# The branch at the end of a kernel: the skipped transfers go to another queue, and the flag is computed earlier

## The chip, the cores and the metric

The kernel runs on one core of a Trainium2 chip. The metric is device time in microseconds (us). The program is one launch with one execution of straight-line code and, at the very end, one branch on a value computed on the device.

## The reference

A gated recurrence over 6080 steps, then two dense layers with a shrink function between them:

```python
sig = 1.0 / (1.0 + np.exp(-f_logit))
f = lower_bound + (1.0 - lower_bound) * sig
for t in range(S):                      # B=4, S=6080, D=256
    h = f[:, t] * h + (1.0 - f[:, t]) * x[:, t]
    y[:, t] = h
h = y.reshape(B * S, D) @ w_in          # 256 -> 2048
g = h - np.tanh(h)
out = g @ w_out                         # 2048 -> 256
```

## The kernel before

`fast()` computes everything with a polynomial for `h - tanh(h)` that holds for small `h`. While it works, ScalarE adds up in `flags` by how much any `h*h` exceeds a bound. At the end `worst` is the maximum of the flags, a product with a column of ones sums it over the partitions, and the sum goes to `flag`. If it isn't zero, `general()` recomputes the output in full. With the given inputs it is zero and `general()` is skipped. Every engine reads the flag and branches.

```python
def end(j):                                     # the last block, in two halves
    for half, slot, r in ((0, 2, 1), (1, 1, 0)):
        nc.vector.tensor_tensor(...)            # last addition, waits for Qd
        turn_out(j, (slot,))                    # VectorE transpose
        send(j, half)                           # four nc.sync.dma_start of 64 KB

def sum_up():
    most = ps_b.tile([P, 2, HB], FP32, name="most", tag="D")
    nc.tensor.matmul(most[0:1, 0, 0:1], lhsT=worst[:], rhs=ones[:], start=True, stop=True)
    nc.scalar.copy(out=flag[:], in_=most[0:1, 0, 0:1])
...                                             # order of the last unit on TensorE:
                                                # Qa, Qb, Qc, Qd (8, 8, 4, 8 products), then `most`
@with_exitstack
def general(ctx):
    ...
    fetch_w(u, raw[:], nc.sync)                 # 16 loads of weights
    fetch(j)                                    # 8 loads of each of 48 blocks, nc.sync
    nc.sync.dma_start(out=out[...], in_=osb[...])   # one store of each block
...
fast()
seen = nc.values_load(flag[:].bitcast(INT32), ...)  # every engine loads the flag
with tc.If(seen != 0, label="general"):
    general()
```

Of the kernel before, what the change touches and what calls it, by code (L numbers as in the profile page):

```python
# [31 lines left out]
def kernel(  # L32
# [25 lines left out]
    nc = tc.nc  # L58
# [18 lines left out]
    NBLK = len(starts)  # L77
# [81 lines left out]
    def recurrence(ctx):  # L159

        natpool = ctx.enter_context(tc.tile_pool(name="nat", bufs=1))
        midpool = ctx.enter_context(tc.tile_pool(name="mid", bufs=1))
        ypool = ctx.enter_context(tc.tile_pool(name="ypool", bufs=2))
        nats, chan, ys = {}, {}, {}

        def fetch(j, parts=(0, 1)):
            t0, nb = starts[j], sizes[j]
            for s in parts:
                nat = natpool.tile([P, TB // H, KC * H], FP32, name=("fn", "xn")[s])
                src = srcs[s][t0 : t0 + nb, :].rearrange(  # L170
                    "(j b) (i c) -> i b j c", b=H, i=G
                )
                for i in range(G):
                    nc.sync.dma_start(
                        out=nat[i * H : (i + 1) * H, 0 : nb // H, :], in_=src[i]
                    )
                nats[j, s] = nat

        def turn(j, s):

            n = sizes[j] // H
            dst = midpool.tile([P, TB // H, KC, H], FP32, name=("fT", "xT")[s])
            nc.vector.transpose(
                out=dst[:, 0:n].rearrange("p j k b -> p (j k b)"),
                in_=nats[j, s][:, 0:n, :].rearrange("p j (a k) -> p j k a", k=KC),
            )
            chan[j, s] = dst[:, 0:n]

        def squash(j):

            u = chan[j, 0]
            nc.scalar.activation(out=u, in_=u, func=AF.Sigmoid, scale=-1.0)

        def forget(j, k):

            f = midpool.tile([P, TB // H, H], FP32, name="f", tag=f"f{k}")
            nc.scalar.activation(
                out=f[:, 0 : sizes[j] // H], in_=chan[j, 0][:, :, k, :],
                func=AF.Identity, scale=nom[:, k : k + 1], bias=1.0,
            )  # L200
            chan[j, "f", k] = f[:].rearrange("p j b -> p (j b)")

        def enter(j, k):

            v = midpool.tile([P, TB // H, H], FP32, name="v", tag=f"v{k}")
            nc.vector.scalar_tensor_tensor(
                out=v[:, 0 : sizes[j] // H], in0=chan[j, 0][:, :, k, :],
                scalar=om[:, k : k + 1], in1=chan[j, 1][:, :, k, :],
                op0=ALU.mult, op1=ALU.mult,
            )  # L210
            chan[j, "v", k] = v[:].rearrange("p j b -> p (j b)")

        def recur(j, k):


            t0, nb = starts[j], sizes[j]
            if j not in ys:
                ys[j] = ypool.tile([P, KC, TB], FP32, name="y")
            y, f, v = ys[j], chan[j, "f", k], chan[j, "v", k]
            cuts = [c for c in range(1, nb) if (t0 + c) % S == 0]  # L220
            for a, e in zip([0] + cuts, cuts + [nb]):
                if (t0 + a) % S == 0:
                    init = 0.0
                else:
                    pn = sizes[j - 1]
                    init = ys[j - 1][:, k, pn - 1 : pn]
                nc.vector.tensor_tensor_scan(
                    out=y[:, k, a:e], data0=f[:, a:e], data1=v[:, a:e], initial=init,
                    op0=ALU.mult, op1=ALU.add,
                )  # L230

        steps = dict(
            tf=lambda j: turn(j, 0),
            tx=lambda j: turn(j, 1),
            sg=squash,
            f0=lambda j: forget(j, 0),
            f1=lambda j: forget(j, 1),
            v0=lambda j: enter(j, 0),
            v1=lambda j: enter(j, 1),
            sc0=lambda j: recur(j, 0),  # L240
            sc1=lambda j: recur(j, 1),
        )
        return fetch, steps, ys, natpool, midpool, nats, chan

    @with_exitstack
    def fast(ctx):
# [8 lines left out]
        fetch, steps, ys, natpool, midpool, nats, chan = recurrence(ctx)  # L255
# [274 lines left out]
        def end(j):  # L530
# [38 lines left out]
            o3=lambda j: finish(j, 3),  # L569
# [26 lines left out]
        for word in around.split():  # L596
            name, u, at = re.fullmatch(r"([a-zA-Z0-9]+)(?:\.(\d))?([+-]\d)?", word).groups()
# [235 lines left out]
        def sum_up():  # L833

            most = ps_b.tile([P, 2, HB], FP32, name="most", tag="D")
            nc.tensor.matmul(
                most[0:1, 0, 0:1], lhsT=worst[:], rhs=ones[:], start=True, stop=True
            )
            nc.scalar.copy(out=flag[:], in_=most[0:1, 0, 0:1])
# [33 lines left out]
        with tc.manual_schedule():  # L873
            nc.vector.memset(zeros[:], 0.0)
            nc.vector.memset(ones[:], 1.0)
            nc.scalar.dma_start(
                out=lb[:], in_=lower_bound.rearrange("(p k) -> p k", k=KC)
            )
            make_identity(nc, ident[:])

            nc.scalar.activation(out=flag[:], in_=ones[0:1, :], func=AF.Sigmoid)
            nc.scalar.activation(
                out=om[:], in_=lb[:], func=AF.Identity, scale=-1.0, bias=1.0
            )
            nc.scalar.activation(out=nom[:], in_=lb[:], func=AF.Identity, bias=-1.0)
            busy = ps_b.tile([P, TB], FP32, name="B", tag="B")
            open_by(before.split())
            for cycle in range(PLAIN + 1, NBLK + 3):
                for name, u, at in turns:
                    j = cycle + at  # L890
                    if not PLAIN <= j < NBLK:
                        continue
                    if u is None:
                        if (name, j) == ("o1", NBLK - 1):
                            tc.mark_branch_hint_location("general", "LikelyTaken")
                            nc.vector.reduce_max(
                                out=worst[:], in_=flags[:], axis=mybir.AxisListType.X
                            )
                        if j == NBLK - 1 and name in ("o4", "otr"):
                            if name == "o4":  # L900
                                sum_up()
                                end(j)
                            continue
                        steps[name](j)
                        if (name, j) == ("o3", NBLK - 1):
                            turn_out(j, (0, 3))
                        if name == "tx" and j + 1 < NBLK:
                            fetch(j + 1)
                        continue
                    steps[name](j * NU + u)  # L910

    @with_exitstack
    def general(ctx):

        fetch, steps, ys = recurrence(ctx)[0:3]
        wpool = ctx.enter_context(tc.tile_pool(name="w", bufs=1))
# [8 lines left out]
        def temp(tag, dtype=FP32):  # L925
            return tpool.tile([P, 2, 2, HB], dtype, name=tag, tag=tag)

        with tc.manual_schedule():
            for u in range(NU):
                for fetch_w, w in ((fetch_w_in, w_in[u]), (fetch_w_out, w_out[u])):  # L930
                    raw = tpool.tile([P, KC * TB], INT64, name="raw", tag="raw")
                    fetch_w(u, raw[:], nc.sync)
                    rounding = to_float32(
                        [(w[:].rearrange("p a b c -> p (a b c)"), lambda a: a)], raw[:],
                        lambda n: temp(dict(e="t", m="q", r="th")[n])[:].rearrange(
                            "p a b c -> p (a b c)"
                        ),
                    )
                    for step in ("ce", "cr", "cx", "cm", "cs", "cb", "cw"):
                        rounding[step]()  # L940
            for j, nb in enumerate(sizes):
                ns = nb // P
                fetch(j)
                for step in ("tf", "tx", "sg", "f0", "f1", "v0", "v1", "sc0", "sc1"):
                    steps[step](j)
                ps = ps_o.tile([P, NQ, D], FP32, name="psO")
                for u in range(NU):
# [43 lines left out]
                                )  # L991
                osb = opool.tile([P, NQ, D], FP32, name="osb")
                nc.scalar.copy(out=osb[:, 0:ns, :], in_=ps[:, 0:ns, :])
                nc.sync.dma_start(
                    out=out[starts[j] : starts[j] + nb, :].rearrange(
                        "(i p) d -> p i d", p=P
                    ),
# [1 line left out]
                )  # L999

    fast()
    seen = nc.values_load(
        flag[:].bitcast(INT32),
        skip_runtime_bounds_check_because="it is only compared with zero",
    )
    with tc.If(seen != 0, label="general"):
        general()


# [30 lines left out]
```

## Time and profile before

| | before |
|---|---|
| time, median of 3 runs | 2337.45 us (2335.92 to 2338.53) |
| span of the profiled run | 2334.7 us |
| TensorE busy | 2318.4 us, 99% |
| last transpose ends | 11.45 us before the end |
| SyncE's last eight issues | 2322.48 to 2329.72 us, two of them over 2 us long |
| SyncE from its branch to its next instruction | 2.48 us |

The body belongs to TensorE; the last 11 us belong to SyncE. The lines that show it stand in the prediction. A `q` after an engine's name marks an instruction that its sequencer handles, and `L1006` is the line of the branch. SyncE *issues* a transfer with one instruction; the transfer has *landed* when its semaphore, a counter on which others wait, is full. A *semaphore step* raises by hand a semaphore that a skipped transfer would have raised. An *instruction packet* is a packet of the DMA queues that the page marks as `instruction`: in the profile before 85 packets of 16 KB on queue 8 (1.39 MB) and 63 of 8 KB on queue 14 (0.52 MB). One that follows an engine's branch is called that engine's *fetch*. TensorE's branch began at 2322.44 us. `L836` is the line of the flag's product: TensorE's sequencer was at the wait ahead of it at 2318.3 us. At its end the program waits for all semaphores and then goes through *drains* and a barrier of all engines.

### The profile page before, as it was taken

The page shows a single profiled execution, that of the slowest core. Times are in us where ns is not written, and L with a number is a line of the kernel's source. Part 1 is how long each engine was busy: PE and PEld are TensorE (multiplying, and loading weights), DVE is VectorE, ACT ScalarE, POOL GpSimd, SP SyncE. Part 2 cuts the span into 40 slices and gives each one's busy share as a digit, 9 for nine tenths or more (in the row PEclk, how much of TensorE's full clock was granted, in tenths as well). Part 3 has the DMA queues.
Part 4 walks back from the last instruction along what each step waited for, and adds up shares of the span by engine and source line. Part 5 has one row for each costly group of instructions (what it writes and reads, how often), then busy time and mean ns, then how long its engine had stood idle before and what let it go on. Part 6 is the DMA issues. An engine that isn't in the chain of part 4 may idle for free.

```text
span 2334.7 us, 28635 instructions
## 1 busy us (share of the span) xinstructions
PE 2318.4 (99%) x10669; PEld 2024.6 (87%) x10669; DVE 2121.2 (91%) x2450; ACT 1800.4 (77%) x2685; POOL 0.7 (0%) x6
## 2 busy tenths in 40 slices
PE   9999999999999999999999999999999999999997
PEld 6888888888888888888888888888888888888886
DVE  8999899998999999998999989999899998999987
ACT  7677777777777777777777777777777777778774
POOL 0000000000000000000000000000000000000000
PEclk9999999999999999999999999999999999999999
DMA  5211111111111211112111121111211111111101
GB/s 172 63 23 35 39 37 28 28 39 35 37 28 28 45 29 37 28 28 46 31 34 28 28 46 36 28 28 30 44 37 28 28 36 37 37 28 28 28 10 29
DMA packets 298564, 85.05 MB, mean 36 GB/s; under 512 B 292016, under 2 KB 294320, under 8 KB 298416
## 3 DMA queue, kind: packets, MB, share of 16 engines
q1 hardware_dynamic: 298272, 83.14, 16.9%
q8 instruction: 85, 1.39, 0.3%
q14 instruction: 63, 0.52, 0.1%
q10 hardware_dynamic: 144, 0.00, 0.0%
HBM read 58.20 MB, written 24.90 MB: 36 GB/s over the span
## 4 chain that ended last, share of the span: by engine, by line
PE 99%; DMA 0%; SPq 0%; DVE 0%; issue 0%; DVEq 0%
PE A L383 27%; PE Qa L466 14%; PE Qb L466 14%; PE D L383 14%; PE Qd L466 14%; PE Qc L466 7%; PE B L383 7%; PE Qc L745 1%; PE Qa L745 1%; PE Qb L745 1%; PE A L678 1%; PE D L678 0%; PE Qd L678 0%; DMA xn<-in_x_dram 0%; PE B L678 0%; PE Qc L678 0%
## 5 line engine op out<-in xcount | busy, mean ns | idle before, releaser
L383 PE MATMUL A<-T,w_in 128*128 128x256 f32 x2208 | 558.8, 379 | 0.0
L383 PEld LDWEIGHTS A<-T,w_in 128*128 128x128 f32 x2208 | 419.5, 190 | 57.0
L427 DVE TENSOR_TENSOR h<-h,q 128x1024 f32<-128x1024 f32 x368 | 437.3, 1219 | 3.1
L421 DVE SCALAR_TENSOR_TENSOR q<-q,t 128x1024 f32<-128x1024 f32 x368 | 439.8, 1215 | 0.0
L414 ACT ACTIVATE q<-t 128x1024 f32<-128x1024 f32 x368 | 382.9, 1053 | 46.3 <-DVE h L427 43.4
L411 ACT ACTIVATE t<-h 128x1024 f32<-128x1024 f32 x368 | 388.6, 1056 | 3.1 <-DVE h L398 0.3
L432 ACT ACTIVATE junk<-t 128x1024 bf16<-128x1024 f32 x368 | 388.2, 1055 | 1.5
L446 DVE TENSOR_TENSOR Tg<-h 128x1024 f32<-128x1024 f32 x368 | 347.8, 945 | 6.3
L466 PE MATMUL Qb<-h,w_out 128*128 128x256 f32 x1472 | 347.7, 379 | 0.0
L466 PEld LDWEIGHTS Qb<-h,w_out 128*128 128x128 f32 x1472 | 279.7, 190 | 38.0
L466 PE MATMUL Qa<-Tg,w_out 128*128 128x256 f32 x736 | 219.0, 379 | 0.0
L466 PE MATMUL Qd<-Tg,w_out 128*128 128x256 f32 x736 | 218.9, 379 | 0.0
L466 PE MATMUL Qd<-h,w_out 128*128 128x256 f32 x736 | 218.9, 379 | 0.0
L466 PE MATMUL Qa<-h,w_out 128*128 128x256 f32 x736 | 218.9, 379 | 0.0
L395 ACT COPY h<-B 128x512 f32<-128x512 f32 x184 | 107.0, 581 | 143.3 <-PE B L383 94.5
L395 ACT COPY h<-A 128x512 f32<-128x512 f32 x184 | 107.2, 583 | 136.7 <-PE A L383 125.3
L398 DVE TENSOR_TENSOR h<-D,r 128x512 f32<-128x512 f32 x184 | 126.8, 689 | 93.6 <-PE D L383 91.3
L398 DVE TENSOR_TENSOR h<-A,r 128x512 f32<-128x512 f32 x184 | 126.2, 686 | 74.6 <-PE A L383 42.5
L395 ACT COPY r<-A 128x512 f32<-128x512 f32 x184 | 107.2, 583 | 106.0 <-PE A L383 106.0
L383 PE MATMUL B<-y,w_in 128*128 128x256 f32 x736 | 188.9, 379 | 0.0
L383 PE MATMUL D<-y,w_in 128*128 128x256 f32 x736 | 188.9, 379 | 0.0
L383 PE MATMUL A<-y,w_in 128*128 128x256 f32 x736 | 188.9, 379 | 0.0
(114 smaller groups left out, 3068.3 us busy)
## 6 DMA issues: line engine op xcount, KB each, us to landing
xn<-in_x_dram SPq DMA_DIRECT2D x184, 128.0 KB, 3.3
fn<-in_f_logit_dram SPq DMA_DIRECT2D x184, 128.0 KB, 3.2
out_dram<-osb SPq DMA_DIRECT2D x180, 128.0 KB, 2.8
raw<-in_moe_w_in_dram SPq DMA_DIRECT2D x8, 512.0 KB, 5.2
raw<-in_moe_w_out_dram SPq DMA_DIRECT2D x8, 512.0 KB, 4.7
fn<-in_f_logit_dram SPq DMA_DIRECT2D x1, 512.0 KB, 6.6
xn<-in_x_dram SPq DMA_DIRECT2D x1, 512.0 KB, 7.4
out_dram<-osb SPq DMA_DIRECT2D x1, 512.0 KB, 2.9
```

What stands on the lines that cost most here:

```text
L383: nc.tensor.matmul(ps[:, c], lhsT=w_in[u][:, slot, c * P : (c + 1) * P], rhs=mixes[j][right], start=start and c == 0, stop=True, skip_grou ...
L395: nc.scalar.copy(out=dst, in_=piece(n, bank))
L398: nc.vector.tensor_tensor(out=piece(n, "h")[:, q], in0=piece(n, bank), in1=piece(n, r), op=ALU.add)
L411: nc.scalar.activation(out=half(n, i, "t"), in_=half(n, i), func=AF.Square)
L414: nc.scalar.activation(out=half(n, i, "q"), in_=half(n, i, "t"), func=AF.Square, scale=RA, bias=RB,)
L421: nc.vector.scalar_tensor_tensor(out=q, in0=q, scalar=RC, in1=t, op0=ALU.add, op1=ALU.mult)
L427: nc.vector.tensor_tensor(out=h, in0=h, in1=q, op=ALU.mult)
L432: nc.scalar.activation(out=junk[:, :, :, 0 : st[n]["hb"]], in_=t, func=AF.Relu, bias=-TINY, accum_out=flags[:, 2 * n + i : 2 * n + i + 1],)
L446: nc.vector.tensor_tensor(out=o, in0=a, in1=b, op=ALU.subtract)
L466: nc.tensor.matmul(acc[j, part][:, r, 0 : st[n]["hb"]], lhsT=w_out[u][:, slot, c * P : (c + 1) * P], rhs=piece(n, right)[:, q, c], start=( ...
L678: nc.tensor.matmul(h[c], lhsT=w_in[u][:, 2 * k + s, c * P : (c + 1) * P], rhs=ys[j][:, k, 0:nb], start=k == 0 and (c == 0 or len(banks) == 2),
L745: nc.tensor.matmul(acc[j][i // 2][:, i % 2].rearrange("p (k m) -> p k m", k=2), lhsT=plain[j, u][:, s, c, i * P : (i + 1) * P], rhs=w_out[ ...
```

## The change

SyncE is to skip no code: all transfers of `general()` go through GpSimd's queue. The flag is to be known sooner: its product stands ahead of the last eight products of TensorE instead of behind them. The branch hint goes.

```diff
-        def fetch(j, parts=(0, 1)):
+        def fetch(j, parts=(0, 1), queue=nc.sync):
...
-                    nc.sync.dma_start(
+                    queue.dma_start(
...
                         if (name, j) == ("o1", NBLK - 1):
-                            tc.mark_branch_hint_location("general", "LikelyTaken")
                             nc.vector.reduce_max(
...
                             if name == "o4":
-                                sum_up()
                                 end(j)
                             continue
+                        if (name, j) == ("o3", NBLK - 1):
+                            sum_up()
                         steps[name](j)
...
-                    fetch_w(u, raw[:], nc.sync)
+                    fetch_w(u, raw[:], nc.gpsimd)
...
-                fetch(j)
+                fetch(j, queue=nc.gpsimd)
...
-                nc.sync.dma_start(                      # the store of a block in general()
+                nc.gpsimd.dma_start(
...
-    with tc.If(seen != 0, label="general"):
+    with tc.If(seen != 0):
```

## The prediction

> **What bounds the kernel now.** I read the page first. TensorE is busy for the whole span and is nearly the whole chain that ended last, so nothing that leaves TensorE's stream as it is can move the body of the time:
>
> ```profile
> span 2334.7 us, 28635 instructions
> PE 2318.4 (99%) x10669; PEld 2024.6 (87%) x10669; DVE 2121.2 (91%) x2450; ACT 1800.4 (77%) x2685; POOL 0.7 (0%) x6
> PE 99%; DMA 0%; SPq 0%; DVE 0%; issue 0%; DVEq 0%
> ```
>
> The change touches only what comes after the last product, so I then read the chain near its end, and the busy time in short windows:
>
> ```profile
> 2318.92 0.88 PE Qc L466 x4
> ...
> 2322.45 0.32 DVE C L535
> 2322.78 0.02 issue
> 2322.80 0.45 DVE osb L512
> ...
> 2323.30:2326.00 2.70, 0.00 (x0) 0.00 (x0) 0.00 (x0) 0.00 (x0) 0.00 (x0) 0.74 0.30 64
> 2326.00:2330.00 4.00, 0.00 (x0) 0.00 (x0) 0.00 (x0) 0.00 (x0) 0.00 (x0) 0.50 0.37 81
> 2330.00:2334.70 4.70, 0.00 (x0) 0.00 (x0) 0.00 (x0) 0.00 (x0) 0.00 (x0) 0.50 0.10 24
> ```
>
> The chain ends with VectorE's last transpose at 2323.25 us, 11.45 us before the span ends, and in the three windows (length, then busy time of TensorE, its weight loads, VectorE, ScalarE, GpSimd; clock; DMA share; GB/s) no engine computes. These 11.45 us are SyncE's: it issues the last output, looks at the flag, branches, and closes the program. The timeline of its queue (start, duration) shows the issues, and the views of the lines of the branch and of the waits show the rest:
>
> ```profile
> 2322.48 0.32 SPq L521 DMA_DIRECT2D out_dram<-osb  x1
> 2322.85 0.44 SPq L521 DMA_DIRECT2D out_dram<-osb  x1
> 2323.34 2.20 SPq L521 DMA_DIRECT2D out_dram<-osb  x1
> ...
> 2327.09 2.14 SPq L521 DMA_DIRECT2D out_dram<-osb  x1
> 2329.27 0.45 SPq L521 DMA_DIRECT2D out_dram<-osb  x1
> ...
> L1002 SPq TENSOR_LOAD <-flag x1: 487/487/487, 2329.8 to 2329.8; - x1
> ...
> L1006 SPq EVENT_SEMAPHORE  x8: 17/17/17, 2332.8 to 2333.3; - x8
> ...
> L1006 PEldq COMPARE_BRANCH  x1: 4127/4127/4127, 2322.4 to 2322.4; - x1
> ...
> L1006 SPq COMPARE_BRANCH  x1: 45/45/45, 2330.3 to 2330.3; - x1
> ...
> SPq L1006 <- SPq L1006: 2.4, 1, 2.4
> ...
> L836 PEldq EVENT_SEMAPHORE  x1: 51/51/51, 2318.3 to 2318.3; - x1
> ```
>
> The tail adds up, by the trace's records of SyncE: eight issues of 64 KB from 2322.48 to 2329.72; load of the flag 2329.78 to 2330.27; branch to 2330.39; 2.43 us of nothing until its first instruction at the branch's target (2332.82); eight steps of semaphores that the skipped transfers would have raised, 0.07 to 0.08 us apart (to 2333.41); eight waits 0.06 us apart (to 2333.9); drains and the barrier (0.75 us) to 2334.66. The last output's semaphore is full at 2331.13, so its landing is hidden behind the jump.
>
> Two of the eight issues take 2.20 and 2.14 us where others take some 0.45. In the DMA records, queue 8 brings two packets of 16 KB at 2323.47 (1.64 us) and 2327.31 (1.53 us), and each slow issue ends 0.4 us after such a packet (2325.54 after 2325.11; 2329.23 after 2328.84). [...] The first packet begins 0.98 us after TensorE's branch, the second 0.7 us after it goes on.
>
> [...] after their branches SyncE lost 2.43 us, ScalarE 2.80, VectorE 3.01 and TensorE 4.1, with a fetch 0.88 to 0.98 us after each; GpSimd, which has nothing to skip now, went on 0.16 us after its branch began. [...] here queue 14's packets are 8 KB and only queue 8's are 16 KB. [...] its sequencer was already at the wait ahead of the flag's product at 2318.3, behind the dispatch of products that ran until 2321.51.
>
> **The change part by part.** (1) *SyncE skips no code.* All 16 weight loads, the 8 loads per block and the store of `general` go to GpSimd. SyncE's branch should then cost what GpSimd's does now, 0.16 us in place of the 2.48 us from the branch's start to the next instruction: minus 2.3. The eight semaphore steps go as well: minus 0.6. But the landing comes out: it is full at 2331.13, whereas SyncE would be at its waits at 2330.5, so 0.6 is lost there. The semaphore that lands last is third of eight in the closing list: 5 waits of 0.062 remain after it, 0.31, then 0.75 to the end. With issues as now: 2331.13 + 0.03 + 0.31 + 0.75 = 2332.2, minus 2.4.
>
> (2) *The flag earlier.* `sum_up` moves ahead of `Qd` of the last unit. `worst` is ready at 2318.3, and `Qc` ends at 2319.80; the one-column product (0.19 us) and ScalarE's copy (0.15 us) make the flag known at about 2320.15 in place of 2321.83, 1.7 us earlier. ScalarE, GpSimd and TensorE look then (TensorE's sequencer runs ahead of its products, as seen). Their jumps are off the end of the path already[...]. Its branch moves from 2322.44 to about 2320.75, so its fetches move to some 2321.75 to 2323.4 and 2325.6 to 2327.15. The first is over when the third issue of the first half begins (2323.34): minus 1.7 there; the second half then begins at about 2324.4, its third issue at 2325.4 probably meets the second fetch and is held until 2327.55. The fourth ends at about 2328.05, against 2329.72: minus 1.7. It lands 1.85 us after it began, as now: 2329.5. If the second fetch is missed as well, the issues end at 2326.4 and land by 2328.
>
> (3) *Cost.* The small product now stands in front of the last eight products: by its two loads and passes, 0.1 to 0.3 us of TensorE, which VectorE's last additions wait for (they start 0.05 us after the last `Qd`). Plus 0.15. GpSimd now jumps (about 2.8 us) and steps semaphores (0.6), from about 2320.75 until 2324.2, before anyone needs it at the barrier. Waits for GpSimd's own transfers may be added to SyncE's closing list: up to 8 by 0.062, 0 to 0.5; I take 0.25. The removed hint saves nothing that I can see: the fetches came 0.9 us after the branches in spite of it.
>
> Sum: landing 2329.5 + 0.15 + 0.03 + 0.31 + 0.25 + 0.75 = 2331.0, against 2334.66: minus 3.7 us.
>
> **Rivals.** *The landing takes over completely, with fetches still in the way.* If TensorE's sequencer doesn't look earlier, or the fetches meet both third issues again, only part (1) is left: minus 2.4, less 0.4 for part (3), so minus 2.0. For it: I know only the two slow issues at the end and some 1.2 to 1.4 us ones in the body. Against it: the wait recorded at 2318.3. *Nothing meets:* minus 5.2. *GpSimd's queue costs something:* [...] GpSimd, which releases the barrier, might come last: plus 0.5 to 2. Nothing in the profile of before can show it, since GpSimd issues nothing there; its branch would have to be 8 us late to matter at the barrier. *SyncE still pays the jump* (if both ways of the branch are laid out for it): then only the earlier issues count, and they hide the landing: about minus 1.5. Against it: GpSimd's 0.16 us for an empty path. *The small product stalls TensorE* by more than a pass (a bank still being read): bank D was free long before; at most plus 1.
>
> **Range and chances.** The measured before is 2337.45, with its runs from 2335.92 to 2338.53, so 1.3 us of noise each way on single runs and perhaps 0.7 on a median. The centre is 2337.45 - 3.7 = 2333.75; I shade it by 0.15 for GpSimd's queue and say 2333.9. The rivals run from -5.2 to about -1, so 2331.5 to 2336.3 holds it 8 times in 10. Two per cent is 47 us, four times the whole tail that the change can touch. Only a broken body (another placement in memory that slows everything, a slower clock) could reach that: 1% for slower, 0.5% for faster.
>
> **What would show it.** In the profile of after: SyncE's instruction after its branch follows within 0.2 us, without the 2.4 us wait and without eight semaphore steps; GpSimd gets them. The flag's copy lies near 2320.0, with TensorE's branch near 2320.7 while products still run. The third issue of the first half takes about 0.5 us, that of the second up to 2.2. The last thing to be waited for is the output's landing, and the span is about 2331. Wrong would be: SyncE's jump still there; TensorE's branch after 2322; GpSimd's records between 2325 and the end on the path; TensorE's 2318.4 us of busy time changed by more than a microsecond, which no step here allows.

## The result, and the profile after

The changed kernel took 2333.65 us (median of 6 runs, 2332.7 to 2334.65) against 2336.56 for the kernel before in all 6 of its runs. The ratio is 0.9986, with a 95% interval of 0.9973 to 0.9999. It is the mean time of one kernel's fast runs over that of the other's in the same rounds, so not quite the ratio of the medians. By the 2% rule that is "same"; by the numbers it is some 3 us less. The predicted time was 2333.9.

The page of the profile after has TensorE's busy time unchanged, as no step touched it:

```profile
span 2332.7 us, 28636 instructions
PE 2318.4 (99%) x10669; PEld 2024.9 (87%) x10669; DVE 2122.5 (91%) x2450; ACT 1800.2 (77%) x2685; POOL 0.7 (0%) x6
```

The span fell by only 2.0 us, and this needs care, because the two profiles didn't begin alike. Busy times in two windows near the start, first before, then after (the columns behind the engines are TensorE's granted clock, DMA share and GB/s):

```profile
6.00:12.00 6.00, 5.57 (x25) 3.94 (x26) 5.55 (x12) 3.90 (x9) 0.00 (x0) 1.00 1.05 364
12.00:18.00 6.00, 6.00 (x29) 4.44 (x29) 5.60 (x8) 5.13 (x9) 0.00 (x0) 1.00 1.20 269
```

```profile
6.00:12.00 6.00, 3.54 (x21) 2.60 (x22) 5.89 (x13) 3.73 (x9) 0.00 (x0) 0.97 1.03 351
12.00:18.00 6.00, 6.00 (x26) 4.99 (x27) 4.32 (x6) 3.91 (x8) 0.00 (x0) 0.75 1.19 252
```

In the profile after, TensorE is busy for 3.54 us in place of 5.57 in the first of these windows, and its clock drops to 0.75 in the second: the profile after is 2 us behind before 20 us are over. The change has no part in that: when I profiled the kernel before a second time, it began in the same way (3.63 us busy, then a clock of 0.72) and was 2.05 us behind its own first profile. So two profiles can't be compared by their spans, and I compare **tails**: from the start of the first of TensorE's last four `Qc` products, which both kernels have, to the end of the span.

```profile
2318.76 0.38 PE L466 MATMUL Qc<-Tg,w_out 128*128 128x256 f32 x1
```

```profile
2320.64 0.38 PE L466 MATMUL Qc<-Tg,w_out 128*128 128x256 f32 x1
```

The tail before is 2334.70 - 2318.76 = 15.94 us, after it is 2332.74 - 2320.64 = 12.09 us (from unrounded records): 3.85 us less. A second profile of each gave 15.50 and 12.46. The mean difference is 3.4 us, close to the 2.9 us between the medians.

The line of the branch in the profile after (its number is 1007 now), and then what SyncE's queue waited for near the end:

```profile
L1007 POOLq EVENT_SEMAPHORE  x4: 17/43/43, 2325.9 to 2326.2; - x4
...
L1007 PEldq COMPARE_BRANCH  x1: 3571/3571/3571, 2323.0 to 2323.0; - x1
...
L1007 SPq COMPARE_BRANCH  x1: 50/50/50, 2330.6 to 2330.6; - x1
```

```profile
SPq L1037 <- PEq L1037: 0.7, 2, 0.5
SPq L1037 <- DMA out_dram<-osb: 0.3, 1, 0.3
```

SyncE's eight semaphore steps at the branch are gone, and so is its 2.4 us wait on itself; its next instruction follows 0.19 us after the branch began. GpSimd has four steps of its own, at 2326, when nobody waits for it. SyncE's wait is now for the landing of the output, 0.3 us. SyncE's last eight issues after:

```profile
2324.69 0.32 SPq L521 DMA_DIRECT2D out_dram<-osb  x1
2325.05 0.50 SPq L521 DMA_DIRECT2D out_dram<-osb  x1
2325.60 0.46 SPq L521 DMA_DIRECT2D out_dram<-osb  x1
2326.11 0.46 SPq L521 DMA_DIRECT2D out_dram<-osb  x1
2326.67 1.12 SPq L521 DMA_DIRECT2D out_dram<-osb  x1
2327.83 1.11 SPq L521 DMA_DIRECT2D out_dram<-osb  x1
2328.99 0.45 SPq L521 DMA_DIRECT2D out_dram<-osb  x1
2329.48 0.46 SPq L521 DMA_DIRECT2D out_dram<-osb  x1
```

The first half has no slow issue left; the second half has two of 1.1 us where the kernel before had one of 2.1 us. By the DMA records, the first of the two ended 0.40 us after the last of three 8 KB packets of queue 14, and only the second ended just after a 16 KB packet (0.38 us).

### The profile page after: what moved, and what is told of

It is laid out like the page before. It is cut to its first block, busy times and chain, and to the rows that moved or that the text cites. A ratio compares the mean times of both kernels' runs of the same rounds, so it can differ in the third digit from the quotient of the medians.

```text
span 2332.7 us, 28636 instructions
## 1 busy us (share of the span) xinstructions
PE 2318.4 (99%) x10669; PEld 2024.9 (87%) x10669; DVE 2122.5 (91%) x2450; ACT 1800.2 (77%) x2685; POOL 0.7 (0%) x6
## 4 chain that ended last, share of the span: by engine, by line
PE 99%; DMA 0%; SPq 0%; DVE 0%; issue 0%
PE A L383 27%; PE Qd L466 14%; PE Qa L466 14%; PE Qb L466 14%; PE D L383 14%; PE B L383 7%; PE Qc L466 7%; PE A L678 1%; PE Qa L745 1%; PE Qc L745 1%; PE Qb L745 1%; PE D L678 0%; PE Qd L678 0%; DMA xn<-in_x_dram 0%; PE B L678 0%; PE Qc L678 0%
```

## The experiments

My theory has two parts. (1) SyncE's jump over 448 transfers costs 2.4 us and eight semaphore steps, and under it the landing of the output was hidden. (2) TensorE's jump brings two instruction packets of 16 KB (1.64 and 1.53 us in the profile before), and an issue of SyncE's that meets one ends only some 0.4 us after it (2.20 and 2.14 us in place of 0.45); an earlier flag moves these fetches out of the way. Rival A: only the jump matters and the slow issues have another cause. Rival B: the parts work only together, or the hint did it. All ten kernels gave correct results. All figures are us; issue end and landing count from the start of `Qc`, "rest" is from the landing to the end.

| run | `Qc` starts | last issue ends | last landing | rest | tail | median time |
|---|---|---|---|---|---|---|
| before | 2318.76 | 10.96 | 12.37 | 3.58 | 15.94 | 2336.56 |
| e10_before_again | 2320.81 | 10.30 | 11.70 | 3.80 | 15.50 | (2338.2, one run) |
| after | 2320.64 | 9.30 | 10.84 | 1.25 | 12.09 | 2333.65 |
| e9_after_again | 2320.68 | 9.80 | 11.20 | 1.25 | 12.46 | 2333.33 |
| e1_queue_only | 2319.47 | 9.09 | 11.60 | 1.25 | 12.85 | 2335.08 |
| e2_early_only | 2320.55 | 9.85 | 11.27 | 3.55 | 14.82 | 2336.93 |
| e3_hint_back | 2319.68 | 9.92 | 11.32 | 1.25 | 12.58 | 2333.79 |
| e4_look_sooner | 2320.73 | 8.92 | 10.33 | 1.25 | 11.58 | 2334.07 |
| e5_tensor_late | 2319.09 | 11.30 | 12.70 | 1.25 | 13.96 | 2334.87 |
| e6_stores_sync | 2320.90 | 9.84 | 11.26 | 2.54 | 13.80 | 2335.44 |
| e7_scalar_queue | 2319.22 | 9.64 | 11.05 | 1.72 | 12.76 | 2335.25 |
| e8_two_queues | 2319.40 | 7.87 | 9.89 | 1.33 | 11.23 | 2334.16 |

`Qc` starts anywhere from 2318.76 to 2320.90, and the same kernel takes nearly both ends of that (before), so medians of four to six runs scatter by about as much as the smaller effects. By the 2% rule every timed run is "same", and of all the intervals of ratios only that of the changed kernel's first six runs lies below 1. The tails are the better measure, but most kernels have one profile only. Repeats of one kernel differ in them by 0.4.

**e1_queue_only: the queue alone.** The kernel before with `nc.gpsimd` for `general()`'s transfers; flag and hint as before.

> Only the queue of the path for large h moves to GpSimd; flag and hint stay as before. Measure the tail in the profile, from the first of the last four Qc products to the end of the span: 15.94 us before, 12.06 us after. My theory: SyncE's jump (2.4 us) and its eight semaphore steps go, the landing of the last output comes out, TensorE's fetches still hold two of the eight issues for about 2.1 us each. Tail about 13.5 us, time about 2.4 us less than before. Rival A (only SyncE's jump matters, the two slow issues have nothing to do with TensorE's branch): tail about 12.1, as after.

The tail is 12.85, which is 2.65 to 3.1 less than before's two profiles; 2.4 was expected. The rest from the landing to the end fell from 3.58 to 1.25. The issues happened to be shorter in this profile (1.09 and 0.94 for the slow ones), but TensorE's second fetch, from 9.28 to 10.24, then met the landing instead: it came 3.0 us after the last issue began, where 1.85 is what before and e9 have. SyncE's waits say so:

```profile
SPq L1036 <- DMA out_dram<-osb: 1.1, 1, 1.1
```

So the first part stands by itself. That a fetch can strike the data as well as the issue is read from this one profile and was not tested.

**e2_early_only: the flag's product alone.** The kernel before with `sum_up()` moved; SyncE still jumps.

> Only the flag's product moves ahead of the last Qd; the transfers stay with SyncE and the hint stays. My theory: TensorE's instruction fetches come 1.5 to 1.7 us sooner, SyncE's eight issues end about 1.7 us sooner, SyncE still jumps for 2.4 us after them, the small product costs 0.2 us: tail 15.94 - 1.5 = about 14.4 us, time about 1.5 us less than before. Rival A: no issue gets faster, tail about 16.1. Rival B (the two parts only work together): tail about 16.

The tail is 14.82: 0.7 to 1.1 less than before, against an expected 1.5. The issues ended at 9.85 in place of 10.96 and 10.30. The jump stays in full, as SyncE's wait shows:

```profile
SPq L1007 <- SPq L1007: 2.4, 1, 2.4
```

Rivals A (16.1) and B (16) miss it by over a microsecond, but the gain is only a little larger than the scatter, so this run alone doesn't settle part (2).

**e5_tensor_late: only TensorE looks later.** The changed kernel, with one product that makes TensorE wait for the last sum of the first half:

```diff
+        def hold(j):
+            last = ps_b.tile([P, 2, HB], FP32, name="last", tag="D")
+            nc.tensor.matmul(last[0:1, 0, 0:1], lhsT=acc[j, "C"][:, <one column of slot 2>],
+                             rhs=ones[:], start=True, stop=True)
...
                                 end(j)
+                                hold(j)
```

> On top of after: one 1-column product on TensorE, which reads the last sum of the first half, stands between the last Qd and TensorE's look at the flag, so that TensorE branches about 1.7 us later while all else stays (its result is not used). My theory: TensorE's two 16 KB fetches fall on the third issue of each half again, as in before, both issues take about 2 us, and the landing comes about 1.5 us later: tail about 13.5 us. Rival A: tail 12.1, no slow issues tied to the fetches.

TensorE's branch moved from 2.32 to 4.32 us after `Qc`, and the 16 KB packets of queue 8 from 3.35 and 6.63 to 5.39 and 9.30, so they are TensorE's. The last issues of each half are the slow ones now:

```profile
2324.49 2.20 SPq L521 DMA_DIRECT2D out_dram<-osb  x1
...
2328.64 1.76 SPq L521 DMA_DIRECT2D out_dram<-osb  x1
```

The tail is 13.96, 1.5 to 1.9 more than after, although only TensorE's look at the flag was moved. Rival A is out. In the first half the fourth issue was struck and not the third: the place depends on when the packet comes.

**The slow issues in all twelve profiles.** I went through every issue by SyncE of inputs of the recurrence and of outputs, from 40 us on, that took over 0.85 us (the usual is 0.3 to 0.75). There are 133, of which 21 are in the tails. In all 133 an instruction packet ended inside the issue, and the issue ended 0.14 to 0.52 us after it, mostly 0.4. In 115 of them the last such packet was one of 16 KB, in 18 one of 8 KB. Of the 6463 other issues, only 203 had the end of a packet inside. This is as near as a trace comes to showing that the packet holds the issue up; it doesn't show by what means, and no trace here shows which DMA engine a packet used.

**e4_look_sooner: the flag sooner still.** After, with two more moves: on VectorE the maximum of the flags goes ahead of the last `s4`, and the transpose of the block before goes behind it; `sum_up()` stands ahead of `Qb` of the last unit. The lines at the old places, which go, are left out here.

```diff
+                        if (name, j) == ("otr", NBLK - 2):
+                            nc.vector.reduce_max(out=worst[:], in_=flags[:], ...)
+                            continue                      # its transpose follows s4 below
...
+                    if (name, j, u) == ("Qb", NBLK - 1, NU - 1):
+                        sum_up()
                     steps[name](j * NU + u)
+                    if (name, j, u) == ("s4", NBLK - 1, NU - 1):
+                        give(NBLK - 2)
```

> On top of after: the maximum of the flags is taken two DVE steps sooner (ahead of s4 and of the transpose of the block before), and the flag's product stands ahead of Qb of the last unit, so TensorE branches near the time that Qb starts. My theory: both of TensorE's 16 KB fetches are over, or nearly, when SyncE issues the first half; no issue of the first half is slow, the second half is held by at most VectorE's 8 KB fetch (0.6 us). Landing 0.5 to 1.2 us sooner than after: tail 10.9 to 11.6 us against 12.06. Rival A: no change, tail 12.0 to 12.1. Rival C (the reordering on VectorE delays the last products): tail measured from Qc the same, but Qc itself starts later against Qa.

The tail is 11.58, as expected, and the second half has no slow issue. The second 16 KB packet (4.03 to 5.27) still caught the second issue of the first half (1.57 us). But the flag's product costs its 0.3 us ahead of `Qc` here. From the start of the eight `Qa` products, e4's tail is 11.58 + 3.77 = 15.35 and after's 12.09 + 3.45 = 15.54, so the gain is 0.2 to 0.6 us against the two profiles of after, and the times (2334.07) don't show it.

**e3_hint_back: the hint.** After, with the hint and its label put back.

> After, with the branch hint and its label put back. My theory: the hint does nothing here, tail 12.06 +- 0.3 us, the jumps of ScalarE, VectorE and TensorE as long as in after. Rival (the hint had cost something, or had saved something): tail off by 0.5 us or more, and a fetch at another time.

The tail is 12.58, within 0.12 of e9's and 0.5 of after's; issues, fetches and jumps come at the same places. One issue took 2.11 us. There is no sign that the hint did anything, but half a microsecond couldn't be told from the scatter.

**e6_stores_sync: does any skipped code cost?** After, with the 48 stores of `general()` back on SyncE (`nc.sync.dma_start` there), its 400 loads left with GpSimd.

> After, with the 48 stores alone (of 448 transfers of the path for large h) back on SyncE. It tells whether SyncE pays for any skipped code or for the distance. If for the distance: [...] its branch costs 0.2 to 0.4 us, plus up to eight semaphore steps of 0.07 us: tail 12.1 to 12.7 us. If for any skipped code: 2.4 us of jump, but the landing is hidden behind it again: tail about 13.5 to 14.

SyncE's branch took 0.19 us to the next instruction, as with nothing to skip; there was no jump's wait. So not any skipped code costs: 48 transfers cost nothing at the branch, 448 cost 2.4 us. That fits the distance; no number in between was tried. Both forecasts of the tail failed, though: it is 13.80. The eight semaphore steps are back. The third of them waits for the landing; five more steps and twelve closing waits follow it (1.15 us), where after has five waits left at that point (0.30). These account for 0.85 us of the 1.29 by which the rest grew. A pause of 0.35 us ahead of the first drain, where after has 0.04, and that drain itself, 0.13 us in place of 0.01, account for the remaining 0.4; I have no cause for them.

```profile
L1007 SPq EVENT_SEMAPHORE  x8: 17/17/17, 2331.5 to 2332.5; - x8
```

**e7_scalar_queue: another queue for the skipped path.** After, with `nc.scalar` in place of `nc.gpsimd` in `general()`.

> After, with ScalarE's queue in place of GpSimd's for the path for large h. It tells whether GpSimd's queue itself costs anything. My theory: ScalarE jumps already and has 2 us to spare, so tail 12.06 +- 0.3 us. Rival [...]: this one is faster than after by 0.5 us or more. Rival (semaphore steps come back to SyncE's side or ScalarE becomes last at the barrier): slower by 0.5 or more.

The tail is 12.76. SyncE doesn't jump here either (0.19 us), but the transfers on ScalarE's queue use the same semaphores as those on SyncE's (number 100 for both in the profiles before and after), so SyncE keeps the eight steps, and five of them follow the one that waits for the landing: a rest of 1.72 in place of 1.25. That 0.47 is what GpSimd's queue brings beyond "SyncE skips no code". It has a small cost too: from SyncE's first drain to the end the seven other profiles with GpSimd's queue have 0.87 us (e6 1.00, with its long drain), those without it 0.79 to 0.80; GpSimd's clearing of the semaphores takes 178 ns there in place of 135.

**e8_two_queues: the issues split.** e4, with the four issues of the first half of the last output on ScalarE's queue.

> On top of e4_look_sooner: the four issues of the first half of the last output go out from ScalarE's queue (ahead of its look at the flag), those of the second half from SyncE's, as before. My theory: neither half waits for the other's issues, SyncE's four end about 6.5 to 7.5 us after Qc began in place of 8.92, the landing comes 1 to 2 us sooner; ScalarE now looks at the flag late, and its jump (2.6 to 3.1 us) ends about 9.0 to 9.5, which becomes the end: tail 9.9 to 10.5 us against 11.58. Rival [...]: tail 11 or more.

The tail is 11.23: outside my theory's 9.9 to 10.5 and inside the rival's "11 or more", which was for the case that both queues are held up at once. They were: the second issue of ScalarE (1.58 us) and that of SyncE (0.83) ended together, 0.43 us after a 16 KB packet. ScalarE's jump ended at 10.27 and not by 9.5: it waited for the first half's sum and then issued until 6.9. SyncE's issues had gaps now: the third and the fourth of its half each waited until a transfer from ScalarE's queue had landed, whose semaphore they reuse (full at 2325.71 and 2326.94; they were issued at 2325.72 and 2326.95). The third wait in the view comes before these, for a transfer of SyncE's own.

```profile
SPq L521 <- DMA out_dram<-osb: 2.2, 3, 0.9
```

The time, 2334.16, isn't better than after's.

**e9_after_again and e10_before_again: the scatter.**

> The changed kernel once more, unaltered: how far the tail scatters between profiles. From the runs so far (three profiles with the same order of work: issues ending 9.30, 9.92, 9.64 us after Qc began) I expect a tail of 12.1 to 12.6 us. If it lies outside, differences of half a microsecond between single profiles say nothing, and only those of a microsecond and more stand.

> The kernel before once more, unaltered: tail 15.94 us in its first profile. I expect 15.0 to 16.2: the two slow issues vary with how long TensorE's fetches take (1.0 to 1.9 us so far), the jump of 2.4 us and the eight semaphore steps don't.

Both lie inside. No version beats the changed kernel's time by more than the scatter. Only e8's tail is shorter by more than that: from the first of the last eight `Qa` products it is 11.23 + 3.77 = 15.00, 0.5 to 0.9 less than after's two, in a single profile.

## Why the prediction was right

*Time and range.* 2333.9 was said, 2333.65 was measured, well inside 2331.5 to 2336.3. That they are so close is in part luck: the prediction took off 3.55 from 2337.45, the median of three runs, and with all six the kernel before has 2336.56, so that 2.91 was measured; a base 0.9 too high and a step 0.6 too large nearly cancel. In the profile the sum ended at 2331.0, a tail of 2331.0 - 2318.76 = 12.24; the two profiles have 12.09 and 12.46.

*SyncE skips no code.* Right in each item: its branch takes 0.19 us (0.16 said), the eight steps are gone, and the landing, hidden before, sets the end. From the landing to the end 1.25 us were measured; the terms of the sum make 1.34, with the 0.25 for GpSimd's waits that didn't come (see the cost). By itself this part was said to bring 2.4; e1 has 2.65 to 3.1, within the scatter.

*The flag earlier.* That SyncE's issues take longer when TensorE's fetches meet them, and that an earlier flag moves these fetches, was right (in e5 the slow issues, of 2.20 and 1.76 us, came where the packets had moved to, and each of the 133 slow issues ended 0.14 to 0.52 us after an instruction packet); by what means a packet holds an issue up was not shown. The size was not right. The term "minus 1.7" for the end of the issues was taken from one profile of before that had both slow issues above 2 us. With the second one, before ends them at 10.96 and 10.30, after at 9.30 and 9.80: 1.1 on the mean. Also, "its third issue ... is held" named the wrong one: it was the first two in after and the second in e9. And it reckoned with TensorE's packets alone, whereas the first slow issue in after ended with the 8 KB packets. The landing still came where the sum had it (10.89 after `Qc` began; 10.84 in after, 11.20 in e9), by other issues than those named: that is luck. The forecast of where a packet strikes was too fine.

*The branch of TensorE* came 2.3 us after `Qc` began, where 2.0 had been said: ScalarE, GpSimd and TensorE took 0.83 to 0.85 us to load the flag in place of 0.47 to 0.48. They now load it while TensorE multiplies, but that alone isn't the cause: in e4 they do so too and took 0.47 to 0.49. In the traces the DMA engines were 92 to 97% busy with the output of the block before during each of the slow loads, and idle in e4's. But one load of ScalarE's in e8 took only 0.55 at 96%, so the cause stays open.

*The cost.* The product ahead of `Qd` delays the last product by 0.32 us (it starts 2.69 after `Qc` began, against 2.37), where 0.15 was said. GpSimd's extra waits were said to cost 0.25; there are four, and they are over before the landing, so they cost nothing. Drains and barrier were said to take 0.75 and took 0.87, of which 0.07 is GpSimd's queue. These errors nearly cancel.

*The rivals.* The jump was not still there, GpSimd's queue cost 0.07 us and not 0.5 to 2, and GpSimd was done at 2326.5, 5 us before the barrier. (That GpSimd releases the barrier is read from the profile before: its last step, at 2334.60, is followed by those of the four other engines at 2334.64 and 2334.65.) The small product didn't wait for its bank: in the profile before the last read of `D` ended at 2301.59, some 20 us ahead of it, and in after the product takes 0.12 us of the chain that ended last. That the hint saved nothing held as far as e3 can tell.

## What to carry to other kernels

A branch that is skipped wasn't free here for an engine whose own code in it is long. From the start of the branch to the next instruction, SyncE took 2.48 us over 448 transfers (before) and 0.19 over 48 (e6) or none (after); in the profile before ScalarE took 2.85, VectorE 3.08 and TensorE 4.18, and GpSimd, with nothing to skip, 0.16 (3.00 in after, with the 448). It counted on SyncE, the engine that closes the program (e1: a tail 2.65 to 3.1 us shorter); so put the skipped transfers on an idle engine with semaphores of its own (a rest of 1.25 us with GpSimd's queue, 1.72 with ScalarE's). Let the engines that must jump do so early, since their instruction fetches can hold up the issues of the last output, as they did here (up to 2.20 us in place of some 0.45). When an effect is a few microseconds in two milliseconds, compare the stretch that the change touches from an instruction that both kernels share, and profile each kernel twice.
